# A GLU block's down projection in seven half-size products, beside a spectral filter: one edit to a tuned kernel

## The chip, the cores and the metric

The kernel runs on one core of a Trainium2 chip. The metric is device time in microseconds (us) of one execution. Below, PE is the matmul engine, PEld its weight loads, DVE the vector engine, ACT the scalar engine, POOL the GpSimd engine and SP the sync engine, which here only starts DMAs. "SPq" and "ACTq" are the DMA-starting parts of those engines.

## The reference, cut to what matters

The output is the sum of three things: the input `x` (2048 rows of 512), a spectral filter of its layer norm, and a gated MLP of the same layer norm.

```python
def _A_ref(x, w_r, w_i):
    X = jnp.fft.rfft2(x.astype(jnp.float32), axes=(-2, -1)) * (w_r + 1j * w_i)
    return jnp.fft.irfft2(X, s=(S, D), axes=(-2, -1)).astype(jnp.bfloat16)

def _B_ref(x, w_gate, w_up, w_down):      # 512 -> 1792 -> 512
    h = _gelu(jnp.einsum("bsd,df->bsf", x, w_gate)) * jnp.einsum("bsd,df->bsf", x, w_up)
    return jnp.einsum("bsf,fd->bsd", h, w_down)

xn = _layernorm(A_x)
return A_x + _A_ref(xn, A_w_r, A_w_i) + _B_ref(xn, B_w_gate, B_w_up, B_w_down)
```

## The kernel before, in words

**Rows.** The 2048 rows lie in SBUF as `x_sb`, 16 row blocks `j` of 128 rows by 512 columns (bf16). Four blocks form a chunk `b` (0 to 3). `x_sb` is also the accumulator: the MLP's result and the filter's result `y` are each added into block `j`, and when both are in (`part_done`, twice per block), two DMAs on SP write the block out.

**The MLP.** A loop over chunks and, in each, over 14 slices `fc` of the hidden dimension. `gate` (L685) runs four matmuls of 128x512 into a PSUM bank, ACT applies gelu into `gl` (L688); `up` (L700) runs four more into another bank, and DVE multiplies the two into `hT` (L706), of which there are two, for odd and even chunks. `down(b, jj)` (L738) takes one row block: 14 matmuls with a 128x128 piece of `hT` as weights and 512 columns of `wd` moving, all into one bank, then one DVE add into `x_sb` (`add_to`, L640). The downs of chunk b−1 run inside chunk b, after fc 2, 5, 8 and 11; those of chunk 3 come after everything else. The very last block is split into two column halves (`last_down`, L721), each with its own adds and outputs: first half, then second half.

**The filter.** It is spread through the MLP as small stages: D and A (forward transforms, with a round trip through DRAM: `scr1`, read back as `tv`), B (L570) and the product with the loaded filter `W` (DVE, L581), C (L595, another round trip through DRAM: `scr2`, read back as `vv` into `arena`), E (L619) and F (L649). `W` comes in eight steps `s` of eight 64 KB loads, half on POOL's queue and half on SP's, into a ring of four places (`load_W`); `keep_256` (L559, POOL) saves one column of each. E of block j is copied out by ACT (L626), POOL overwrites one row of it (L628), F reads it, ACT copies F's bank out (L655), and four DVE operations of 256 columns (L665 to L668, a quartet below) make `y`, which a fifth (L640) adds into `x_sb`.

**The order.** Each engine works strictly through its own list, written in program order. What belongs where is set by hand: a counter of "hooks" goes up after every gate, every up, and three times in each down; `at(h, call)` puts a small stage at hook h, and `later`/`flush` put DVE work off until after the next up. B starts at hook 60 and every 4.6 hooks, E at 113 and every 2.2 hooks, F four hooks after E. The helper `op` derives semaphore waits from named keys: a reader waits for the last writer of a key, a writer for its readers too. The block's accumulator has one key, `("acc", j)`. `take` hands out PSUM banks (eight of 512 f32 columns) by a planner's own estimate of when each is free; the real waits come from the keys.

**The end.** After chunk 3's fc there are four downs in a row with a few F stages between; the last adds are followed by output DMAs, on SP and, for half of the last block, on ACT.

Of the kernel before, what the change touches and what calls it, by code (L numbers as in the profile page):

```python
# [13 lines left out]
S = 2048  # L14
# [200 lines left out]
def bass_parallel_sum__spectral_gfnet__glu_gated_geglu__prompt_kernel(  # L215
# [27 lines left out]
    with ExitStack() as es:  # L243
        def sb(name, shape, dt):
            return es.enter_context(nc.sbuf_tensor(name, shape, dt))
# [23 lines left out]
        ev1 = cmx[:, 0:1024].rearrange("p (a c) -> p a c", a=2)  # L269
        xn = cmx[:, 1024:3072].rearrange("p (a d) -> p a d", a=4)  # L270

        W = [[sb("W%d_%d" % (k, i), [P, 2, 2, 258], BF16) for i in range(4)] for k in range(2)]
        w256 = sb("w256", [P, 2, 2, NJ], BF16)
        early = sb("early", [P, 8192], F16)
        xs = [early[:, 512 * i:512 * i + 512] for i in range(8)]
# [10 lines left out]
        zt = [late[:, 512 * i:512 * i + 512].rearrange("p (a t) -> p a t", a=4) for i in range(NZ)]  # L286
        eo = [late[:, 2048 + 512 * i:2560 + 512 * i] for i in range(2)]
        uvt = [late[:, 3072 + 512 * i:3584 + 512 * i] for i in range(2)]
        ys2 = [late[:, 4096 + 512 * i:4608 + 512 * i] for i in range(2)]
        TVK = [("tv", m, r) for m in range(4) for r in range(2)]  # L290
        z256 = late[:, 5120:7168]
        row = sb("row", [32, 64], BF16)
# [6 lines left out]
        mhalf = sb("mhalf", [P, 4], F32)  # L299
        vpe = sb("vpe", [P, NJ], F32)  # L300
        rstd = sb("rstd", [P, NJ], F32)
        dumm = sb("dumm", [P, 512], F16)
        warm_o = sb("warm_o", [P, 1], F32)

# [3 lines left out]
        def bank(i):  # L308
            return psum[:, i * 512:(i + 1) * 512]
# [11 lines left out]
        def take(n, dur, hold=None, ops=1):  # L321
            i = min(range(9 - n), key=lambda i: max(free[i:i + n]))
            pt[0] += dur
            if hold is None:
                act_t[0] = max(act_t[0], pt[0] + 0.25) + 0.2 + 0.43 * n
                end = act_t[0]
            else:
                end = pt[0] + hold
            for k in range(i, i + n):
                free[k] = end  # L330
            return i

        def dma(eng, dst, src, r=(), w=()):
            return op(eng, lambda e: e.dma_start(dst, src), r=r, w=w, dma=True)  # L334
# [293 lines left out]
            op("pool", lambda e: e.tensor_copy(z[0:1, 1, :], z256[0:1, P * j:P * j + P]), r=["z256"], w=[zk])  # L628

        done = {}  # L630

        def part_done(j):

            done[j] = done.get(j, 0) + 1
            if done[j] == 2:
                for b in range(2):
                    dma("sp", ov[b, :, j, :], x_sb[64 * b:64 * b + 64, j, :], r=[("acc", j)], w=[("out", j, b)])

        def add_to(j, src, r, cs=slice(0, D), key=None):
            op("dve", lambda e: e.tensor_tensor(x_sb[:, j, cs], src, x_sb[:, j, cs], ALU.add), r=r + [("acc", j), ("x", j, 0), ("x", j, 1)], w=[("acc", j)])  # L640

        def unit_F(j):
            bk = take(1, 0.23)

            def fn(e):
                z = zt[j % NZ]
                ins = None
                for a in range(4):
                    ins = e.matmul(bank(bk)[:, a * P:(a + 1) * P], z[:, a, :], gm[:, a, :], start=(a == 0), stop=(a == 3), skip_group_check=True)  # L649
                return ins  # L650

            op("pe", fn, r=["gm", ("zt", j % NZ)], w=[("ps", bk)])
            o2 = eo[j % 2]
            ok = ("eo", j % 2)
            op("act", lambda e: e.activation(o2, bank(bk), ACT.Copy), r=[("ps", bk)], w=[ok] + (TVK if j < 2 else []))  # L655
            uv = uvt[j % 2]
            uk = ("uv", j % 2)
            ys = ys2[j % 2]
            yk = ("ys", j % 2)
            u2 = uv.rearrange("p (i h c) -> p i h c", i=2, h=2)  # L660
            neg = ys[:, ::-1].rearrange("p (i h c) -> p i h c", i=2, h=2)[:, :, 0, :]
            pos = ys.rearrange("p (i h c) -> p i h c", i=2, h=2)[:, :, 0, :]

            def fin():
                op("dve", lambda e: e.tensor_tensor(uv[:, 0:256], o2[:, 0:256], o2[:, 256:512], ALU.add), r=[ok], w=[uk + (0,)])  # L665
                op("dve", lambda e: e.tensor_tensor(uv[:, 256:512], o2[:, 0:256], o2[:, 256:512], ALU.subtract), r=[ok], w=[uk + (1,)])
                op("dve", lambda e: e.tensor_tensor(pos, u2[:, :, 0, :], u2[:, :, 1, :], ALU.add), r=[uk + (0,), uk + (1,)], w=[yk + (0,)])
                op("dve", lambda e: e.tensor_tensor(neg, u2[:, :, 0, :], u2[:, :, 1, :], ALU.subtract), r=[uk + (0,), uk + (1,)], w=[yk + (1,)])  # L668

                add_to(j, ys, [yk + (0,), yk + (1,)])  # L670
                part_done(j)
            later.append(fin)

# [36 lines left out]
            else:  # L710
                mult()

        def last_down(bk):
            for c in range(2):
                cs = slice(256 * c, 256 * c + 256)
                bc = (bk + c) % 8

                def fn(e, cs=cs, bc=bc):
                    ins = None
                    for fc in range(NFC):  # L720
                        ins = e.matmul(bank(bc)[:, 0:256], hT[1][:, fc, 3 * P:4 * P], wd_sb[:, fc, cs], start=(fc == 0), stop=(fc == NFC - 1))  # L721
                    return ins
                op("pe", fn, r=[("wd", fc) for fc in range(NFC)] + [("hT", 1, fc, 3) for fc in range(NFC)], w=[("ps", bc)])
                add_to(NJ - 1, bank(bc)[:, 0:256], [("ps", bc)], cs)
                for b, eng in ((0, "sp"), (1, "act")):
                    dma(eng, ov[b, :, NJ - 1, cs], x_sb[64 * b:64 * b + 64, NJ - 1, cs], r=[("acc", NJ - 1)], w=[("out", NJ - 1, b, c)])
            for _ in range(3):
                hook()

        def down(b, jj):  # L730
            j = 4 * b + jj
            bk = take(1, 0.0, 1e9)

            def part(f0, f1):
                def fn(e):
                    ins = None
                    for fc in range(f0, f1):
                        ins = e.matmul(bank(bk), hT[b % 2][:, fc, jj * P:(jj + 1) * P], wd_sb[:, fc, :], start=(fc == 0), stop=(fc == NFC - 1))  # L738
                    return ins
                pt[0] += 0.217 * (f1 - f0)  # L740
                op("pe", fn, r=[("wd", fc) for fc in range(f0, f1)] + [("hT", b % 2, fc, jj) for fc in range(f0, f1)], w=[("ps", bk)])

            if j == NJ - 1:
                return last_down(bk)
            part(0, 5)
            hook()
            part(5, 10)
            hook()
            part(10, 14)
            free[bk] = pt[0] + 1.2  # L750

            add_to(j, bank(bk), [("ps", bk)])
            part_done(j)
            hook()
# [4 lines left out]
        def at(h, *calls):  # L759
            plan.setdefault(int(h), []).extend(calls)  # L760
# [5 lines left out]
        def hook(fl=True):  # L766
            for f, *a in plan.pop(hk[0], []):
                f(*a)
            hk[0] += 1
            if fl:  # L770
                flush()
# [3 lines left out]
            at(10 + 2 * i, (load_late, wd_sb[:, f0:f1, :], wdv[:, f0:f1, :], [("wd", fc) for fc in range(f0, f1)]))  # L775
        at(18, (load_late, be[:], c_be.ap(), ["be"]))
        at(19, (load_late, mm[:], c_mm.ap(), ["mm"]))
        for s, h0 in enumerate((22, 30, 53, 59, 65, 70, 74, 79)):
            for i, t in enumerate(load_W(s)):
                at(h0 + i // 2, t)  # L780
            at(h0 + 9 if s > 1 else 53 + s, (keep_256, s))
        cmv = c_cm.ap().rearrange("p (h r c) -> p h r c", h=NJ, r=2)
        for i, h0 in enumerate((52, 62, 71, 80)):
            hs = slice(4 * i, 4 * i + 4)
            at(h0, (load_late, cm[:, hs], cmv[:, hs], [("cm", 2 * i), ("cm", 2 * i + 1)], (["ev1"], ["ev1", ("xn", 0)], [("xn", 1), ("xn", 2)], [("xn", 2), ("xn", 3)])[i]))
        at(60, (load_late, gm[:], c_g.ap().rearrange("p (a c) -> p a c", a=4), ["gm"]))
# [20 lines left out]
                at(h + 7, (mini, 0))  # L807
            at(h + 8 + (4 if m < 1 else 0), (load_tv, m))
        for g in range(9):
            h = int(60 + 4.6 * g)  # L810
            if g < 8:
                at(h, (unit_B, g))
            if g > 0:
                at(h, (unit_C, g - 1))
                if g > 1:
                    at(h, (load_vv, g - 2))
            if g == 1:
                at(h, (mini, 1))
            if g == 8:
                at(h - 2, (mini, 4))  # L820
                at(h, (mini, 2))
        at(100, (mini, 3))
        at(101, (load_vv, 7))
        for j in range(NJ):
            at(113 + 2.2 * j, (unit_E, j))
            at(117 + 2.2 * j, (unit_F, j))

        def trans1(j):
            for i, eng in enumerate(("dve", "act")):
# [39 lines left out]
        trans(0, (2, 3), (2, 3), "act")  # L869
        gate(0, 5, (0, 1))  # L870
        up(0, 5, (0, 1))
        NH = 6
        for b in range(4):
            for fc in range(NFC):
                jjs = (2, 3) if b == 0 and fc < NH else (0, 1, 2, 3)
                gate(b, fc, jjs)
                hook(False)
                up(b, fc, jjs)
                flush()
                hook()  # L880
                if b > 0 and fc in (2, 5, 8, 11):
                    down(b - 1, (fc - 2) // 3)
        for jj in range(4):
            down(3, jj)
        assert not plan
        pr.wait_all_dma("sp", [ev for k, ev in pr.writer.items() if k[0] == "out"])

# [49 lines left out]
```

## Time and profile before

| | |
|---|---|
| median of 4 runs | 188.79 us (188.01 to 189.7) |
| the profiled execution's own time | 189.7 us |
| its span, first to last instruction | 187.9 us |
| mean granted PE clock | 0.998 |
| PE, DVE, ACT, POOL busy | 96%, 59%, 47%, 21% of the span |
| chunk 3's loop, about | 132 to 171.5 us |
| last output DMA landed | 187.42 us |

The profiled execution's time has 1.8 us around the span that no instruction fills. Lines of the profile name a line of the kernel, an engine and operation, and the tiles as out<-in; "x28" is a count. Matmul records overlap, because their ends are modelled, and a few are missing: L738 has 197 records of 210. So a matmul's price is the distance from one start to the next, not its duration. Where an answer says "[0.84 <-PE ps L721]", the engine was idle for 0.84 us before, until that instruction released it.

### The profile page before, as it was taken

The numbers are of one execution on the slowest core, as the hardware profiler recorded it, in microseconds if no ns is written. First come the engines' busy times: TensorE is split into PE (matmuls) and PEld (weight loads), VectorE is DVE, ScalarE is ACT, GpSimd is POOL, SyncE is SP. The second block draws the span as 40 slices with busy tenths as digits, with TensorE's granted clock in tenths as the row PEclk, the third lists the DMA queues.
The fourth block names the chain that finished last, engine by engine and source line by source line (L and its number), as shares of the span: only waits on it lengthen the run. The fifth ranks groups of instructions, "written<-read, shape, count | busy, mean of one in ns | idle before, by whom it ended". The sixth has DMA issues, their size and how long they took to land.

```text
span 187.9 us, 3460 instructions
## 1 busy us (share of the span) xinstructions
PE 179.6 (96%) x1271; PEld 95.3 (51%) x1284; DVE 110.7 (59%) x262; ACT 88.9 (47%) x143; POOL 39.7 (21%) x90
## 2 busy tenths in 40 slices
PE   7879999999999999999999999999999999999991
PEld 2358755565655444444444444444555555555460
DVE  3476989998362242446645554523259879699520
ACT  1334547766656431455734555513265566654100
POOL 2110081824000007534656200000011111110000
PEclk9999999999999999999999999999999999999999
DMA  4999999798989149756799997420002212211111
GB/s 116 267 247 283 292 272 308 200 184 138 194 112 174 32 100 138 155 143 163 154 223 158 181 221 169 115 57 0 0 3 56 56 45 70 58 37 24 28 42 42
DMA packets 24977, 24.71 MB, mean 132 GB/s; under 512 B 2832, under 2 KB 22800, under 8 KB 24704
## 3 DMA queue, kind: packets, MB, share of 16 engines
q1 hardware_dynamic: 20992, 18.24, 45.3%
q0 software_dynamic: 1968, 5.14, 11.8%
q10 hardware_dynamic: 2000, 1.11, 2.1%
q8 instruction: 10, 0.16, 0.4%
q14 instruction: 7, 0.06, 0.1%
HBM read 18.19 MB, written 6.29 MB: 130 GB/s over the span
## 4 chain that ended last, share of the span: by engine, by line
PE 80%; DVE 8%; DMA 6%; issue 2%; SPq 2%; POOL 1%; ACT 0%; DVEq 0%
PE ps L738 24%; PE ps L700 22%; PE ps L685 21%; DMA wu<-in_B_w_up_dram 5%; DVE st L380 3%; SPq L334 2%; PE ps L595 2%; PE ps L649 2%; PE ps L619 2%; PE ps L570 1%; DVE hT L706 1%; PE ps L402 1%; DMA out_dram<-x_sb 1%; PE ps L471 1%; PE ps L721 1%
## 5 line engine op out<-in xcount | busy, mean ns | idle before, releaser
L700 PE MATMUL ps<-xnT,wu 128*128 128x512 f16 (+1 forms) x248 | 58.6, 359 | 1.1 <-DMA wu<-in_B_w_up_dram 1.0
L685 PE MATMUL ps<-xnT,wg 128*128 128x512 f16 (+1 forms) x248 | 58.6, 359 | 0.7 <-DMA wg<-in_B_w_gate_dram 0.6
L706 DVE TENSOR_TENSOR hT<-ps,gl 128x512 bf16<-128x512 f32 (+1 forms) x62 | 39.4, 636 | 33.7 <-PE ps L700 29.2
L688 ACT ACTIVATE gl<-ps 128x512 bf16<-128x512 f32 (+1 forms) x62 | 34.5, 556 | 46.4 <-PE ps L685 45.6
L738 PE MATMUL ps<-wd,hT 128*128 128x512 bf16 x197 | 46.5, 379 | 0.9 <-issue 0.3
L685 PEld LDWEIGHTS ps<-xnT,wg 128*128 128x128 bf16 x248 | 23.2, 98 | 22.2 <-issue 1.2
L700 PEld LDWEIGHTS ps<-xnT,wu 128*128 128x128 bf16 x248 | 23.3, 98 | 21.7 <-DMA wu<-in_B_w_up_dram 1.9
L738 PEld LDWEIGHTS ps<-wd,hT 128*128 128x128 bf16 x210 | 19.7, 98 | 21.9 <-issue 1.0
L640 DVE TENSOR_TENSOR x_sb<-ps,x_sb 128x512 bf16<-128x512 f32 (+1 forms) x17 | 11.2, 659 | 21.0 <-PE ps L738 17.5
L337 POOL DMA_DIRECT2D W<-in_A_w_r_dram x32 | 18.6, 612 | 13.0 <-PE ps L685 7.8
L628 POOL COPY tv<-tv 1x128 bf16<-1x128 bf16 x16 | 4.5, 284 | 55.2 <-ACT tv L626 55.2
L581 DVE TENSOR_TENSOR early<-early,W 128x1024 bf16<-128x1024 f16 x16 | 10.3, 687 | 7.2 <-ACT early L576 7.2
L655 ACT ACTIVATE tv<-ps 128x512 bf16<-128x512 f32 x16 | 9.5, 595 | 9.8 <-PE ps L649 9.8
L380 DVE BATCH_NORM_STATS2 st<-x_sb 128x6 f32<-128x512 bf16 x16 | 10.5, 681 | 3.9 <-DMA x_sb<-in_A_x_dram 3.9
L447 ACT ACTIVATE early<-ps 128x512 f16<-128x512 f32 x16 | 9.5, 595 | 5.4 <-PE ps L443 5.4
L576 ACT ACTIVATE early<-ps 128x1024 f16<-128x1024 f32 x8 | 8.2, 1023 | 6.5 <-PE ps L570 6.5
L626 ACT ACTIVATE tv<-ps 128x512 bf16<-128x512 f32 x16 | 9.6, 598 | 3.0 <-PE ps L619 3.0
L479 ACT ACTIVATE early<-ps 128x1024 f16<-128x1024 f32 x8 | 7.9, 1022 | 4.6 <-PE ps L474 3.8
L388 POOL TENSOR_TENSOR rstd<-vpe,mhalf 128x4 f32<-128x4 f32 (+1 forms) x5 | 4.5, 901 | 23.7 <-DVE vpe L387 23.7
L600 ACT ACTIVATE early<-ps 128x1024 bf16<-128x1024 f32 x8 | 8.2, 1020 | 0.8 <-PE ps L595 0.8
L392 DVE TENSOR_SCALAR cmx<-x_sb,ag,rstd 128x512 f16<-128x512 bf16 x16 | 6.1, 420 | 2.1 <-POOL rstd L388 2.1
L640 DVE TENSOR_TENSOR x_sb<-tv,x_sb 128x512 bf16<-128x512 bf16 x16 | 6.8, 424 | 0.6
(75 smaller groups left out, 145.4 us busy)
## 6 DMA issues: line engine op xcount, KB each, us to landing
W<-in_A_w_r_dram POOLq DMA_DIRECT2D x32, 64.2 KB, 3.6
W<-in_A_w_i_dram SPq DMA_DIRECT2D x32, 64.2 KB, 5.1
tv<-scr SPq DMA_DIRECT2D x8, 256.0 KB, 5.2
scr<-early SPq DMA_DIRECT2D x8, 256.0 KB, 4.2
arena<-scr SPq DMA_DIRECT2D x8, 256.0 KB, 5.7
out_dram<-x_sb SPq DMA_DIRECT2D x30, 64.0 KB, 2.0
scr<-early SPq DMA_DIRECT2D x14, 128.0 KB, 3.6
x_sb<-in_A_x_dram SPq DMA_DIRECT2D x6, 256.0 KB, 11.8
```

Of the source, the lines that this page charges most:

```text
L337: op(eng, lambda e: e.dma_start(dst, src), w=list(keys) + list(also), dma=True, after=[("pe", pr.cnt["pe"])])
L380: op("dve", lambda e: e.bn_stats(st[:, j, :], x_sb[:, j, :]), r=[("x", j, 0), ("x", j, 1)], w=[("st", j)])
L447: op("act", lambda e: e.activation(x4.rearrange("p (a c r) -> p a c r", a=2, r=4), bank(bk).rearrange("p (a r c) -> p a c r", a=2, r=4), A ...
L581: op("dve", lambda e, k=k: e.tensor_tensor(pp[i][k], xc[i], W[k][g % 4][:, :, :, 0:256], ALU.mult), r=[("xc", i)] + [key for c in range(2) ...
L626: op("act", lambda e: e.activation(z, bank(bk).rearrange("p (a c) -> p a c", a=4), ACT.Copy, scale=SC_E), r=[("ps", bk)], w=[zk] + (TVK if ...
L640: op("dve", lambda e: e.tensor_tensor(x_sb[:, j, cs], src, x_sb[:, j, cs], ALU.add), r=r + [("acc", j), ("x", j, 0), ("x", j, 1)], w=[("ac ...
L655: op("act", lambda e: e.activation(o2, bank(bk), ACT.Copy), r=[("ps", bk)], w=[ok] + (TVK if j < 2 else []))
L685: ins = e.matmul(bank(bg)[:, 0:n], wg_sb[:, dc, fc * P:(fc + 1) * P], xnT[:, dc, c0:c0 + n], start=(dc == 0), stop=(dc == 3))
L688: op("act", lambda e: e.activation(gl[k % 3][:, 0:n], bank(bg)[:, 0:n], ACT.Gelu_apprx_tanh), r=[("ps", bg)], w=[("gl", k % 3)])
L700: ins = e.matmul(bank(bu)[:, 0:n], wu_sb[:, dc, fc * P:(fc + 1) * P], xnT[:, dc, c0:c0 + n], start=(dc == 0), stop=(dc == 3))
L706: op("dve", lambda e: e.tensor_tensor(hT[b % 2][:, fc, h0:h0 + n], bank(bu)[:, 0:n], gl[k % 3][:, 0:n], ALU.mult), r=[("ps", bu), ("gl", k ...
L738: ins = e.matmul(bank(bk), hT[b % 2][:, fc, jj * P:(jj + 1) * P], wd_sb[:, fc, :], start=(fc == 0), stop=(fc == NFC - 1))
```

## The change

The down projection of chunks 2 and 3 is done in another way; chunks 0 and 1 keep `down`. A chunk's rows are cut in two halves of two blocks, the hidden dimension in two halves of seven fc, and the 512 output columns in two halves. A 2x2 block product needs eight half products; the identity used here needs seven, with sums of the operands: four sums of `wd` (`T`, once), four sums of `hT` (`S`, once per chunk), and sums of the results. This is done for p = 0 and 1, the two blocks of a half.

- `product(b, p, step)`: seven matmuls of 256 columns per step, seven steps. Two PSUM banks `bx` and `by` are held over all seven. After step 0 ACT copies bx to by; after step 3 it copies by to bx. Steps 1 and 4 end in a DVE add of a column half into `x_sb`; steps 2 and 3 in a DVE add of bank and `x_sb` into a new f32 tile `tw` ("base"); steps 5 and 6 in a DVE add of bank and `tw` into `x_sb`.
- Chunk 2's 14 steps stand one after each fc of chunk 3 (p = 0, then p = 1). Chunk 3's 14 steps stand at the end, p = 0 and 1 in turn within each step. `last_down` goes.
- `sums_T` at hooks 92 to 98, `sums_S` of chunk 2 at 100 to 108, of chunk 3 after fc 7 to 13. The `W` ring becomes one tile, whose place `T` takes over; `S` takes over the place of `early`, `xnT` and `cmx`. In chunks 2 and 3 the fc are taken in the order 0, 7, 1, 8, and so on, so that both halves of a sum come early.
- `y` is no longer added by DVE: POOL starts a DMA of 128 KB from `ys` to `x_sb` that accumulates, two hooks after the quartet. `ys` has four buffers instead of two. Between a block's base and the end of its products its `y` add is held back ("locked").
- The accumulator's key is split by column half. Chunk 3's outputs are written per half: 14 DMAs of half width on SP and 2 on ACT.
- Hooks: W loads of s = 2, 3 come at 34 and 40 instead of 53 and 59, the others 2 to 4 hooks earlier, B starts at 58, E at 105 and every 2.6 hooks, F 3.5 hooks after E.

```diff
-        W = [[sb("W%d_%d" % (k, i), [P, 2, 2, 258], BF16) for i in range(4)] for k in range(2)]
+        wring = sb("wring", [P, 8 * 1032], BF16)
+        W = [[wring[:, 1032 * (4 * k + i):1032 * (4 * k + i) + 1032].rearrange("p (r h c) -> p r h c", r=2, h=2) for i in range(4)] for k in range(2)]
+        T = [wring[:].bitcast(F16)[:, 1792 * k:1792 * k + 1792].rearrange("p (f c) -> p f c", f=7) for k in range(4)]
...
+        def sums_S(b, f0, f1, ks):
...
+            for k in ks:
+                a, b2, o, r = ((A(1, 0), A(1, 7), ALU.add, hk(0, 1) + hk(7, 1)),
+                               (ssum(b, 0, f0, f1), A(0, 0), ALU.subtract, s_keys(b, 0, f0, f1) + hk(0, 0)),
+                               (A(0, 0), A(1, 0), ALU.subtract, hk(0, 0) + hk(0, 1)),
+                               (A(0, 7), ssum(b, 1, f0, f1), ALU.subtract, hk(7, 0) + s_keys(b, 1, f0, f1)))[k]
...
+        def product(b, p, step):
...
+            bx, by = wb[p]
+            bk = (bx, bx, by, by, bx, by, by)[step]
...
+                for f in range(7):
+                    ins = e.matmul(o, st_(f), mv(f), start=(f == 0 and step in (0, 5)), stop=(f == 6), skip_group_check=True)
...
+            def out_half(j, hh):
+                if last:
+                    for bb, eng in ((0, "sp"), (1, "act" if step == 6 else "sp")):
+                        dma(eng, ov[bb, :, j, 256 * hh:256 * hh + 256], x_sb[64 * bb:64 * bb + 64, j, 256 * hh:256 * hh + 256], r=[("acc", j, hh)],
...
+            def copy(dst, src):
+                return op("act", lambda e: e.activation(bank(dst)[:, 0:256], bank(src)[:, 0:256], ACT.Copy), r=[("ps", src)], w=[("ps", dst)], after=war(("ps", dst)))
+
+            def base(t, j, *after):
+                locked[j] = []
+                op("dve", lambda e: e.tensor_tensor(t, o, x_sb[:, j, 256:512], ALU.add), r=rk + [("acc", j, 1), ("x", j, 0), ("x", j, 1)], w=[("tw", p, j == jA)],
...
+            if step == 0:
+                copy(by, bx)
+            elif step == 1:
+                add_to(jA, o, rk, 0)
+                out_half(jA, 0)
+            elif step == 2:
+                base(t12, jA)
+            elif step == 3:
+                base(t22, jB, copy(bx, by))
+            elif step == 4:
+                add_to(jB, o, rk, 0)
+                out_half(jB, 0)
+            elif step == 5:
+                add_to(jB, o, rk + [("tw", p, False)], 1, t22)
+                out_half(jB, 1)
+                release(jB)
+            else:
+                add_to(jA, o, rk + [("tw", p, True)], 1, t12)
+                out_half(jA, 1)
+                release(jA)
...
-                add_to(j, ys, [yk + (0,), yk + (1,)])
+                at(hk[0] + 2, (add_y,))
+
+            def add_y():
+                if j in locked:
+                    locked[j].append(add_y)
+                    return
+                op("pool", lambda e: e.dma_start(x_sb[:, j, :], ys, accum_op=ALU.add), r=[yk + (0,), yk + (1,), ("x", j, 0), ("x", j, 1)] + acc(j),
+                   w=acc(j), dma=True)
                 part_done(j)
...
-        for s, h0 in enumerate((22, 30, 53, 59, 65, 70, 74, 79)):
+        for s, h0 in enumerate((20, 27, 34, 40, 61, 66, 70, 75)):
...
-            h = int(60 + 4.6 * g)
+            h = int(58 + 4.6 * g)
...
-            at(113 + 2.2 * j, (unit_E, j))
-            at(117 + 2.2 * j, (unit_F, j))
+            at(105 + 2.6 * j, (unit_E, j))
+            at(108.5 + 2.6 * j, (unit_F, j))
...
+            for n, fc in enumerate(range(NFC) if b < 2 else [7 * (i % 2) + i // 2 for i in range(NFC)]):
...
-                if b > 0 and fc in (2, 5, 8, 11):
-                    down(b - 1, (fc - 2) // 3)
-        for jj in range(4):
-            down(3, jj)
+                if b in (1, 2) and n in (2, 5, 8, 11):
+                    down(b - 1, (n - 2) // 3)
+                if b == 3:
+                    product(2, n // 7, n % 7)
+                    for call in S3.get(n, ()):
+                        sums_S(3, *call)
+        for step in range(7):
+            for p in range(2):
+                product(3, p, step)
```

## The prediction

> **What bounds the kernel now.** I read the page first (busy shares, slices, chain of waits), then the windows of the last third, then the order of time at the end, then the groups by form for prices.
>
> ```profile
> PE 179.6 (96%) x1271; PEld 95.3 (51%) x1284; DVE 110.7 (59%) x262; ACT 88.9 (47%) x143; POOL 39.7 (21%) x90
> ...
> DVE  3476989998362242446645554523259879699520
> ...
> PE 80%; DVE 8%; DMA 6%; issue 2%; SPq 2%; POOL 1%; ACT 0%; DVEq 0%
> ```
>
> A busy PE alone proves little, but the chain agrees: four fifths of it is PE, the rest mostly the start. The DVE slices show where the second limit is near: 9s in the last quarter, over chunk 3.
>
> ```profile
> 146.00:158.00 12.00, 11.95 (x86) 6.62 (x85) 9.85 (x30) 7.12 (x14) 1.47 (x5) 1.00 0.23 56
> 158.00:172.00 14.00, 13.89 (x100) 7.75 (x100) 11.97 (x36) 9.32 (x17) 1.68 (x6) 1.00 0.20 48
> ```
>
> Columns: stretch, length, then busy PE, PEld, DVE, ACT, POOL, clock, DMA share. PE has no holes at full clock; DVE is 82% and 86% busy. So PE work taken out here is time won, as long as DVE keeps up.
>
> ```profile
> 174.51 6.21 PE L738 MATMUL ps<-wd,hT 128*128 128x512 bf16 x28
> ...
> 180.55 3.22 PE L721 MATMUL ps<-wd,hT 128*128 128x256 bf16 x28
> ...
> 182.28 0.42 DVE L640 TENSOR_TENSOR x_sb<-ps,x_sb 128x256 bf16<-128x256 f32 x1 [0.84 <-PE ps L721]
> 182.74 3.16 ACTq L334 DMA_DIRECT2D out_dram<-x_sb  x2
> 184.94 0.42 DVE L640 TENSOR_TENSOR x_sb<-ps,x_sb 128x256 bf16<-128x256 f32 x1 [2.23 <-DMA out_dram<-x_sb]
> ```
>
> Order of time (start, length). Matmuls overlap, so the slot is (length − one)/(n − 1): (6.21 − 0.379)/27 = 0.216 us for 512 columns, (3.22 − 0.272)/27 = 0.109 us for 256. PE's last slot ends at 183.61. The last DVE add comes only at 184.94: it waits for the first half's output DMA, since both halves share one key. The last output lands at 187.42, 3.81 after PE; the span closes 0.48 later.
>
> **The change, part by part.**
>
> *Products (won).* A chunk's down projection takes 56 slots of 0.216 = 12.08 us; in chunk 3, 42 of them and 28 of 0.109 = 12.12. After: 7 products × 7 matmuls × 2 row pairs = 98 slots of 0.109 = 10.70. Two chunks: 24.20 − 21.40 = **2.80 us** off PE. Weight loads double per column; in the 28 half-size slots each load (98 ns) hid under 109 ns, so nothing is added. A rule speaks against this. The Trainium skill, "TensorE: Matmul & The Clock Gate", section "Back-to-back issue gap", puts a sustained stream of load and matmul at about 81 ns for 128 columns and 131 ns for 512: on a straight line, an estimate of 98 ns for 256, so 98 × 98 ns = 9.6 against 56 × 131 ns = 7.3, and each chunk would *lose* 2.3 us. This trace has 0.216 and 0.109 for the same tiles; the rows decide.
>
> *DVE (moved and added).*
>
> ```profile
> L706 DVE TENSOR_TENSOR hT<-ps,gl 128x512 bf16<-128x512 f32 x50 | 34.3, 688 | 31.1 <-PE ps L700 27.3 <-ACT gl L688 2.2 <-PE ps L685 1.1
> L581 DVE TENSOR_TENSOR early<-early,W 128x1024 bf16<-128x1024 f16 x16 | 10.3, 687 | 7.2 <-ACT early L576 7.2
> L640 DVE TENSOR_TENSOR x_sb<-tv,x_sb 128x512 bf16<-128x512 bf16 x16 | 6.8, 424 | 0.6
> L665 DVE TENSOR_TENSOR tv<-tv 128x256 bf16<-128x256 bf16 x16 | 4.6, 286 | 0.7 <-ACT tv L655 0.5
> L640 DVE TENSOR_TENSOR x_sb<-ps,x_sb 128x256 bf16<-128x256 f32 x2 | 0.8, 425 | 3.1 <-DMA out_dram<-x_sb 2.2 <-PE ps L721 0.8
> ```
>
> (Busy us, mean ns, idle before.) Operand sums are 16-bit tensor_tensor like L581 and L665: 0.687 for 1024 columns, 0.42 for 512, 0.285 for 256; on that line 1792 columns are 1.1. T: 4 × 1.1 = 4.4. S: 4 × (0.687 + 0.42 + 0.285) = 5.6 per chunk. Product adds: 12 × 0.425 = 5.1 per chunk for 2.7 before. The y adds go: −6.8. Net +13.6 us of DVE. T and chunk 2's S fall into 122 to 134 us, where DVE is busy 4.25 of 12: hidden. Chunk 3 is where cover is thin. Per fc PE needs 8 × 0.216 + 7 × 0.109 + about 0.44 for E and F, some 3.0 us; for the six fc where S(3) runs I count 18.0. DVE in those: six hT (4.1), seven y quartets (8.1), five adds (2.1), S (4.4): 18.8 by mean durations, 16.7 by starts, since in the order of time hT is followed after 0.60 and a quartet takes 1.05. So DVE is 93 to 104% full: a lag of 0 to 0.8 us. Behind a late DVE stand first the hT banks, six now where seven were; with 4.3 groups an fc a bank comes round after 6/4.3 × 3.0 = 4.2 us, of which its up, the hand-over and hT use 1.8, so PE feels a lag above about 2.3. Next is the tail (chunk 3's products, nothing else on PE). Counted from its start DVE ends the last hT at 0.13, the quartet at 1.2, the last add at 1.6, S at 2.7, two adds at 3.7, and then waits for step 2 until 4.0: some 0.4 to spare before step 3. I take **+0.2**.
>
> *y by DMA.* 16 accumulating transfers of 128 KB on POOL; none is in the trace.
>
> ```profile
> gm<-c_g POOLq DMA_DIRECT2D x1, 128.0 KB, 2.9
> ```
>
> That is the nearest row: same queue, size and partitions, 2.9 us to landing. Bounds: 2.3 (the quickest 64 KB W load on POOL) and 5.8 (twice, as the destination is read too); I take 3.5, nearer to the row. A gain below that is excluded by none but does nothing. Behind the waiting POOL instruction stand only the z copies (L628) of later E, due three hooks later, about 3 us: covered. Who waits for a landing: row 9 (y issued after step 1's add, row base at step 2, one fc later: 3.1 us, of which 0.7 goes before the issue) leaves 2.5 for the transfer, so DVE stands 1.0 at 3.5; and row 15 in the tail, which leaves about 5.5. The first adds to DVE's lag and is worked off in part over the four fc left: **+0.3** for PE. The Trainium skill, "SBUF — State Buffer", section "Who interferes with whom", says that a VectorE op with two SBUF inputs shuts out a GpSimd op that reads SBUF for its whole length, so each issue could slip by one op, up to 0.69. The 16 z copies took 279 to 349 ns beside such quartets: no such slip here, at most 0.07. By the rule row 9 would cost 0.4 more; I leave it in the range.
>
> *ScalarE copies between banks.* 8 of 128x256, like the 383 ns gelu of that size: 3.1 us. In chunk 3 each has an fc to finish. In the tail PE does the other row pair meanwhile: 7 × 0.109 = 0.764. A hand-over costs 0.20 from the last slot to the reader's start (182.08 to 182.28), 0.38 or 0.425 for the copy or add, 0.06 back: 0.64 to 0.69. It fits by 0.08. **+0.1**; if it missed by 0.1 everywhere, four steps × two pairs, +0.8.
>
> *The end.* Halves get their own keys, so the wait of 184.94 goes (183.61 + 0.2 instead). But SP now issues 14 half-size outputs, two per row half.
>
> ```profile
> L334 SPq DMA_DIRECT2D out_dram<-x_sb x32: 466/526/816, 141.2 to 185.4; - x32
> ```
>
> A pair takes about 0.51 + 0.60 = 1.1 on SP (min/median/max above). From step 4 four pairs fall due every 0.764 us but take 1.1, so SP is 1.1 behind when step 6's last one is due, 0.66 after PE: it starts 1.75 after PE's end and lands 1.8 later, 3.55 against 3.81. **−0.25**. With issues of 0.3 it would be −1.1, with 0.66 each +0.8.
>
> *Moved W loads, earlier B and E.* B's first unit comes one gate and up (1.73) earlier: 76.0 instead of 77.74. It waits for the last tv load, which landed at 75.94 (issued 69.84, 6.1). That is on time with nothing left over; the W loads of s=2,3 that now run at about 49 to 62 instead of 72 to 84 could delay the spectrum's stores before it, but DMA stood nearly idle at 62 to 64, and the four tv pairs took 4.3 to 4.6 and 5.9 to 6.2 at any load: +0.1, bound +1.5. E's first unit waits for the last vv load: 9.84 us after C(7) starts, and by the new order E starts 10.9 after it: covered by 1.1. The SP order (row, then vv) is unchanged there.
>
> *Sum.* −2.80 + 0.2 + 0.3 + 0.1 − 0.25 + 0.1 = **−2.35**. The profiled execution's span is 187.9, with 1.8 around it (189.7): it would be 185.55 and 187.35. That run is 0.9 above the median of the four, so I take the difference from the median: 188.79 − 2.35 = **186.4 us**.
>
> **Rivals.**
>
> *R1, the accumulate lands late (slower).* Place: row 9's base in DVE's queue, and row 15's in the tail. With D us to landing the loss is D − 2.5 less some 1.7 that banks and later fc absorb for row 9, and D − 5.5 for row 15, against a gain of 2.85 without either wait and DVE's lag: 2D − 9.7 = 2.85, so it decides from D = 6.3. For: POOL's loads took 6.5 to 8 us while the DMA engines were full (90 to 107 us), and an accumulate is unknown. Against: here DMA is 0.2 busy and 2.9 is the row. At 7.5 the loss is 5.3, so 188.8 − 2.85 + 5.3 = 191.2.
>
> *R2, the gain turns into waits, no change.* DVE over 100% in chunk 3 (sums on every fc, in-order waits for the product's end) and SP's backlog at 0.66 an issue: +0.8 lag into the tail, +0.8 hand-overs, +0.3 at B instead of my small terms, SP +0.8: −2.80 + 0.8 + 0.8 + 0.3 + 0.8 = −0.1, about 188.4 at the worst, 188.0 as its middle. For: 93 to 104%. Against: chunk 3 before ran at 86% without a hole in PE.
>
> *R3, the end is fully won.* Issues on SP overlap, no stall: −2.80 − 1.1 = −3.9: 184.9.
>
> *That the half-size products save nothing* (the rule above) is a fourth: +4.5, 193; the 28 slots of 0.109 leave it 2 in 100, counted with R1.
>
> **How the numbers follow.** Main case 0.50, own range 185.4 to 187.4; R3 0.12; R2 0.20; R1 with the fourth 0.18. A measurement of this kernel (188.0 to 189.7 over four runs) can hardly tell less than 1%, so the bounds are 186.9 and 190.7. Faster: R3 and three quarters of the main case, 0.49. Slower: nearly all of R1, 0.16. Same: the rest, 0.35. The range 184.8 to 190.0 leaves out R1's larger part (0.15) and a little below.
>
> **What would show it.** Right: 98 slots of 0.109 in the last 10.7 us of PE, gate and up unchanged, no DVE wait on a DMA over 1 us, last landing about 3.5 after PE. Wrong: product slots above 0.12; DVE base (x_sb into tw) waiting for the y DMA by several us; holes before the steps of the tail above 0.1; PE waiting before the first B (tv) or E (vv). The prediction falls if landings of the y DMA pass 6 us, or if DVE's lag reaches the hT banks.

## The result, and the profile after

The changed kernel takes 188.28 us (median of 35 runs, 187.3 to 194.06), the kernel before 188.91 (56 runs, 187.95 to 189.91): a ratio of 0.9969, with a 95% interval of 0.9955 to 0.9983. That is 0.6 us less (0.3 to 0.85), where 2.35 less was predicted. The sign is right, the size is a quarter of the forecast. Two of the 35 runs were slow ones with a lower PE clock (190.59 us at 0.988 and 194.06 at 0.977, the others 0.992 or more); here and below such runs count in the medians and not in the ratios.

The profiled execution took 189.13 us, with a span of 187.24 (187.9 before). First the page: busy shares, DVE by slices, and the chain of waits by engine.

```profile
PE 176.5 (94%) x1346; PEld 102.3 (55%) x1354; DVE 121.0 (65%) x289; ACT 91.8 (49%) x151; POOL 53.3 (28%) x106
...
DVE  3566999997452242355635556998687678797750
...
PE 73%; DMA 11%; DVE 7%; SPq 2%; issue 2%; ACT 1%; POOL 1%; ACTq 0%; DVEq 0%
```

PE lost 3.1 us of busy time, but its share of the chain fell from 80% to 73%, while DMA rose from 6% to 11%. So some of the time that PE no longer works is now spent waiting for transfers. DVE's busy time grew by 10.3 us. The sum of its operations' durations grew by 13.2, where 13.6 was predicted; neighbouring operations overlap in the record. Its slices over chunk 3 have 6 to 9, as before.

Where DMA came in is seen in the order of time (start, length) around the first B unit, L573:

```profile
74.32 1.03 PE L836 MATMUL ps<-xnT,wu 128*128 128x512 f16 x4
...
77.23 0.41 PE L573 MATMUL ps<-tv,be 64*64 64x256 f16 x8 [1.89 <-DMA tv<-scr]
```

The four matmuls of `up` fill their slots until 74.32 + 4 × 0.216 = 75.19. B starts at 77.23, 2.05 later, released by the last `tv` load, which landed at 76.89. PE shows about 0.09 at every switch to these 64x64 tiles, so the wait is 1.95 us. Before, this place had no wait.

The second place is the end, in the order of time, and then SP's own queue from the same stretch:

```profile
171.29 3.22 PE L720 MATMUL ps<-wd,hT 128*128 128x256 bf16 x28
172.99 0.29 DVE L797 TENSOR_TENSOR tv<-tv 128x256 bf16<-128x256 bf16 x1 [1.17 <-DMA x_sb<-tv]
174.40 3.23 PE L720 MATMUL ps<-wring,xnT 128*128 128x256 f16 x28
...
180.52 1.69 PE L720 MATMUL ps<-wd,cmx 128*128 128x256 bf16 x14
181.94 1.26 ACTq L337 DMA_DIRECT2D out_dram<-x_sb  x2
182.25 0.42 DVE L649 TENSOR_TENSOR x_sb<-ps,tw 128x256 bf16<-128x256 f32 x1 [0.34 <-PE ps L720]
```

```profile
178.88 6.51 SPq L337 DMA_DIRECT2D out_dram<-x_sb  x10
```

The products do what they should: a slot is (3.22 − 0.272)/27 = 0.109 us, and 28 slots from 171.29 end at 174.35, where the next 28 begin at 174.40. PE's last slot ends at 180.52 + 14 × 0.109 = 182.05 and the last add at 182.67. But SP is still starting output DMAs: ten of them, the first at 178.88, the last at 184.80, so 5.92/9 = 0.66 us from one to the next. The last one lands at 186.70, 4.65 after PE's end, where it was 3.81 before.

The two profiled spans in one sum (us):

| | before | after | difference |
|---|---|---|---|
| span start to the first D matmul | 20.80 | 20.11 | −0.69 |
| from there to PE's last slot, without the wait before B | 162.81 | 159.99 | −2.82 |
| wait before the first B | 0 | 1.95 | +1.95 |
| PE's last slot to the last landing | 3.81 | 4.65 | +0.84 |
| last landing to the end of the span | 0.48 | 0.54 | +0.06 |
| span | 187.9 | 187.24 | −0.66 |

The first row is not the change's: the instructions there are the same, and it varied from 19.57 to 20.80 over the profiles of this study. The wait before B varies too: with these hooks it was 1.95, 0.67, 1.31, 0.54, 1.26 and 1.03 in six profiles (the change and five experiments below), a mean of 1.1. With that mean and without the first row the sum is −2.8 + 1.1 + 0.9 = −0.8, against −0.6 by medians.

### The profile page after: what moved, and what is told of

It reads as the page before. It is cut to its first block, busy times and chain, and to the rows that moved or that the text cites. A ratio compares the mean times of both kernels' runs of the same rounds, so it can differ in the third digit from the quotient of the medians.

```text
span 187.2 us, 3669 instructions
## 1 busy us (share of the span) xinstructions
PE 176.5 (94%) x1346; PEld 102.3 (55%) x1354; DVE 121.0 (65%) x289; ACT 91.8 (49%) x151; POOL 53.3 (28%) x106
## 4 chain that ended last, share of the span: by engine, by line
PE 73%; DMA 11%; DVE 7%; SPq 2%; issue 2%; ACT 1%; POOL 1%; ACTq 0%; DVEq 0%
PE ps L836 19%; PE ps L821 19%; PE ps L720 11%; PE ps L857 11%; DMA wu<-in_B_w_up_dram 4%; DMA tv<-scr 3%; DMA scr<-early 3%; DVE st L383 3%; SPq L337 2%; PE ps L598 2%; PE ps L622 2%; PE ps L779 2%; PE ps L573 1%; DVE hT L842 1%; PE ps L405 1%
## 5 line engine op out<-in xcount | busy, mean ns | idle before, releaser
L857 PE MATMUL ps<-wd,hT 128*128 128x512 bf16 x104 | 24.4, 379 | 0.4
L340 POOL DMA_DIRECT2D wring<-in_A_w_r_dram x32 | 18.5, 611 | 13.3 <-PE ps L857 5.6
L857 PEld LDWEIGHTS ps<-wd,hT 128*128 128x128 bf16 x112 | 10.8, 98 | 12.4 <-issue 0.2
L649 DVE TENSOR_TENSOR x_sb<-ps,x_sb 128x512 bf16<-128x512 f32 (+1 forms) x16 | 8.8, 553 | 9.6 <-PE ps L857 9.3
L805 POOL DMA_DIRECT2D x_sb<-tv x16 | 13.5, 863 | 3.9 <-DVE tv L798 2.5
L584 DVE TENSOR_TENSOR early<-early,wring 128x1024 bf16<-128x1024 f16 x16 | 10.3, 687 | 5.9 <-ACT early L579 5.9
L383 DVE BATCH_NORM_STATS2 st<-x_sb 128x6 f32<-128x512 bf16 x16 | 10.6, 680 | 3.3 <-DMA x_sb<-in_A_x_dram 3.3
L562 POOL COPY w<-wring 128x4 bf16<-128x4 bf16 x16 | 3.9, 251 | 20.1 <-DMA wring<-in_A_w_r_dram 11.4
```

The lines of the kernel that those rows point to most:

```text
L340: op(eng, lambda e: e.dma_start(dst, src), w=list(keys) + list(also), dma=True, after=[("pe", pr.cnt["pe"])])
L383: op("dve", lambda e: e.bn_stats(st[:, j, :], x_sb[:, j, :]), r=[("x", j, 0), ("x", j, 1)], w=[("st", j)])
L584: op("dve", lambda e, k=k: e.tensor_tensor(pp[i][k], xc[i], W[k][g % 4][:, :, :, 0:256], ALU.mult), r=[("xc", i)] + [key for c in range(2) ...
L805: op("pool", lambda e: e.dma_start(x_sb[:, j, :], ys, accum_op=ALU.add), r=[yk + (0,), yk + (1,), ("x", j, 0), ("x", j, 1)] + acc(j), w=ac ...
```

## The experiments

The theory behind the first experiments had three parts: products −2.8; B, set at hook 58, waits for `tv`, and the W loads moved to hooks 34 and 40 are what delays `tv`; SP's rate of issue ends the kernel late. The rivals: B at 58 is too early at any load; the end is bound by something other than SP (the adds, the write itself); DVE is so full that the gain is lost there unless the `y` adds stay off it. All ratios are to the kernel before, on the same chip.

**The W loads late again (`e1_w_late`).** All loads of `W` back at the old hooks, B still at 58.

```diff
-        for s, h0 in enumerate((20, 27, 34, 40, 61, 66, 70, 75)):
+        for s, h0 in enumerate((22, 30, 53, 59, 65, 70, 74, 79)):
...
-            at(h0 + 9 if s > 3 else 47 + s, (keep_256, s))
+            at(h0 + 9 if s > 1 else 53 + s, (keep_256, s))
```

> The changed kernel with the W loads and keep_256 at the hooks of the kernel before (W of s=2,3 at 53 and 59 again); B still starts at hook 58. Theory (the early W loads share the DMA engines with the chunk 2 read-back and the last spectrum stores, so the last tv load is late): the 2.05 us that PE stood before the first B falls to 0.3 or less, the stores of group 3 take 2.5 to 3.8 us again instead of 4.8 to 5.3, time about 186.4, ratio to before 0.987. Rival (B at hook 58 is too early for the tv load whatever else runs): PE still stands 1 us or more there, time 187.8 to 188.3.

Measured: 187.89 us, ratio 0.9950 (0.9917 to 0.9982). In its order of time:

```profile
76.43 0.41 PE L573 MATMUL ps<-tv,be 64*64 64x256 f16 x8 [1.11 <-DMA tv<-scr]
```

B still waits: it starts 1.27 us after the slots before it end, 1.18 without the switch of 0.09. The stores ahead of `tv` did get quicker (2.4 to 4.1 us to landing, where the change had 4.8 to 5.3), but `tv` landed at 76.08, after B's turn. So the early loads are not the cause, or not alone: B at 58 is too early without them. Whether they add to it stays open. From the issue of the last stores to the landing of `tv` it takes 10.3, 10.3 and 11.1 us in the three profiles with late loads (the kernel before, `e8_before_split` and this one), and 10.5 to 11.9, mean 11.1, in the ten with early loads: half a microsecond more, but the ranges overlap.

**The last outputs shared with ACT (`e3_out_act`).** The second DMA of each pair goes to ACT's queue in every step.

```diff
-                    for bb, eng in ((0, "sp"), (1, "act" if step == 6 else "sp")):
+                    for bb, eng in ((0, "sp"), (1, "act")):
```

> The changed kernel with one of the two outputs of every row half of chunk 3 issued by ACT instead of SP. Theory (14 half-size outputs at 0.64 us each on SP are what ends the kernel): the last landing comes 2.8 to 3.2 us after PE's last slot instead of 4.65, time about 186.7, ratio 0.988. Rival (the writes themselves, or the engines behind the queues, are the limit): last landing still 4.3 us or more after PE, time 188.0 to 188.4. A third way: ACT's copies between banks stand behind its own DMA issues (0.5 us each) and PE gets holes in the tail, time 187.5 or more with holes of 0.3 us.

Measured: 186.32 us, ratio 0.9865 (0.9835 to 0.9895); run again as `e12_out_act_b`, 186.18 and 0.9852. The order of time at its end, SP and ACT side by side:

```profile
177.55 4.29 SPq L337 DMA_DIRECT2D out_dram<-x_sb  x6
177.56 4.44 ACTq L337 DMA_DIRECT2D out_dram<-x_sb  x6
...
179.19 1.69 PE L720 MATMUL ps<-wd,cmx 128*128 128x256 bf16 x14
...
180.92 0.42 DVE L649 TENSOR_TENSOR x_sb<-ps,tw 128x256 bf16<-128x256 f32 x1 [0.34 <-PE ps L720]
```

PE ends at 179.19 + 14 × 0.109 = 180.72, and the last output lands at 183.42: 2.70 after PE instead of 4.65. Tiles, adds and bytes are the same; only the queue differs. Nor did ACT's own copies suffer from its DMA starts: PE has no gap above 0.06 us between the steps of the tail. SP's rate was the end's bound, worth 1.95 us; by medians (0.9865 and 0.9852 against 0.9969) 2.0 and 2.2.

**`y` added by DVE as before (`e4_y_dve`).** The accumulating DMA becomes the old DVE add.

```diff
-                op("pool", lambda e: e.dma_start(x_sb[:, j, :], ys, accum_op=ALU.add), r=[yk + (0,), yk + (1,), ("x", j, 0), ("x", j, 1)] + acc(j),
-                   w=acc(j), dma=True)
+                add_to(j, ys, [yk + (0,), yk + (1,)])
```

> The changed kernel with y added into x_sb by DVE again (same hooks, same holding back) instead of the accumulating DMA. DVE gets 16 adds of 0.42 us back, 6.8 us. Theory (DVE was near full in chunk 3 and the DMA add is what made room; the DMA itself costs PE nothing): DVE's lag reaches the hT banks or the tail, PE gets 1 to 4 us of holes after 140 us, time 189 to 192. Rival (the DMA add costs by its own waits, DVE has room): no holes, time 187.5 to 188.3.

Measured: 188.12 us, ratio 0.9938 (0.9917 to 0.9958). The windows late in chunk 3 (stretch, length, busy PE, PEld, DVE, ACT, POOL, clock, DMA share, GB/s), first of the change, then of this run:

```profile
156.00:170.00 14.00, 14.00 (x113) 9.22 (x112) 12.45 (x37) 8.66 (x16) 4.97 (x10) 1.00 0.35 63
```

```profile
156.00:170.00 14.00, 14.00 (x110) 8.97 (x108) 13.65 (x41) 8.78 (x16) 1.43 (x4) 1.00 0.08 20
```

DVE is busy 13.65 of 14 us, 97%, and PE still has no hole; nor has it one above 0.25 us anywhere after 78 us. From the first D matmul to PE's last slot, without the wait before B, it takes 159.99 us, the same as in the change. So the theory's holes did not come, DVE could have kept the adds, and moving them to a DMA won nothing on the path. Whether it cost a little is open: the two intervals (up to 0.9958, from 0.9955) just meet.

**The moved hooks alone (`e5_before_moved`).** The kernel before, with only the new hooks of W, of its companion copies and loads, and of B with C and the small stages that follow it.

```diff
-        for s, h0 in enumerate((22, 30, 53, 59, 65, 70, 74, 79)):
+        for s, h0 in enumerate((20, 27, 34, 40, 61, 66, 70, 75)):
...
-            h = int(60 + 4.6 * g)
+            h = int(58 + 4.6 * g)
```

> The kernel before with only the new hooks of the W loads, of keep_256, of the cm loads and of B (58), C and the small stages beside them; downs, adds, E and F as they were. Theory (the new hooks alone make the wait): PE stands 1.3 to 2.3 us before the first B, time about 190.6, ratio 1.009. Rival (the wait comes from the products' or y's part of the change): no wait over 0.3 us, time 188.9.

Measured: 189.62 us, ratio 1.0038 (1.0017 to 1.0059), so +0.7 us; its profile has a wait of 0.54 before B. The hooks alone make the kernel slower, with no product changed. The wait is less than the theory's 1.3 to 2.3 us and more than the rival's 0.3: the profile of the change, with its 1.95, was at the high end of what this wait takes.

**B two hooks later (`e6_b60`), and both repairs (`e7_b60_act`).** B starts at 60 again, and what follows it is moved along; in the second the outputs are shared with ACT as well.

```diff
-            h = int(58 + 4.6 * g)
+            h = int(60 + 4.6 * g)
...
-            at(105 + 2.6 * j, (unit_E, j))
-            at(108.5 + 2.6 * j, (unit_F, j))
+            at(107 + 2.5 * j, (unit_E, j))
+            at(110.5 + 2.5 * j, (unit_F, j))
```

> The changed kernel with B at hook 60 as before, C, the small stages and the last vv load 2 hooks later with it, T and S of chunk 2 one or two hooks later, E at 107 and every 2.5 hooks, F at 110.5 and every 2.5. The early W loads stay. Theory (the chain from the last spectrum stores to the last tv load takes 10.3 to 11.9 us, B at 58 leaves it 10.2): with 1.73 us more PE stands at most 0.2 us before the first B in a typical execution, time about 187.2 to 187.5, 0.8 to 1.1 less than the changed kernel. Rival (the wait is only moved: PE stands as long before E, C or the products instead): time 188.0 to 188.5.

> B at hook 60 as in e6_b60 and the second output of every row half of chunk 3 issued by ACT as in e3_out_act. If both costs are separate they add: 188.3 - 1.0 - 1.95 = 185.3, ratio 0.981. If they overlap, 186.0 or more.

Measured: 187.48 us, ratio 0.9919 (0.9886 to 0.9951), and 186.15 us, ratio 0.9847 (0.9801 to 0.9892). The first is what was expected. The second is not the 185.3 of two costs that add, and which of the two readings holds is taken up again below. First `e6_b60` around B, then `e7_b60_act` in the tail:

```profile
75.95 1.03 PE L836 MATMUL ps<-xnT,wu 128*128 128x512 f16 x4
...
76.91 0.41 PE L573 MATMUL ps<-tv,be 64*64 64x256 f16 x8
```

```profile
171.38 0.29 DVE L797 TENSOR_TENSOR tv<-tv 128x256 bf16<-128x256 bf16 x1 [1.35 <-DMA x_sb<-tv]
```

The wait before B is gone: 75.95 + 0.86 = 76.81, and B at 76.91. But a smaller one came: E and F are later now, so row 15's quartet waits 1.35 us for its buffer. That buffer is one of the four `ys`, and the held-back `y` transfer of row 11 still reads it. Behind the quartet in DVE's queue stands the last S sum, and step 2 of the tail waits 0.36 for it. In the change itself the same DVE wait is 1.17 (shown above) and PE's other row pair hides all but 0.05 of it.

**One hook instead of two, and both again (`e10_b59_act`, `e11_b60_act_b`, `e12_out_act_b`).** B at 59 with outputs shared; and repeats of `e7_b60_act` and `e3_out_act` on one chip.

```diff
-            h = int(58 + 4.6 * g)
+            h = int(59 + 4.6 * g)
```

> The changed kernel with ACT issuing the second outputs and B, C, the small stages and the last vv load one hook later (B at 59, a gate of 0.86 us later); T, S, E and F as in the change. If PE's wait before the first B is a matter of the chain from the last stores (10.3 to 11.9 us, now against 11.1), it falls to 0 to 0.8 us and nothing else moves (the vv load has 0.2 us to spare before E): time about 185.6, between e3_out_act (186.3) and 185.2. If the wait returns before E instead, 186.3 again.

> The kernel of e7_b60_act once more, for a narrower interval: its profile accounts for 187.3 - 2.83 (products) + 0.36 (a hole before step 2 in the tail) - 1.11 (end) = 183.7 us of span, 185.5 us of time, where four runs gave 186.15. If the two costs add, 185.3 to 185.8; if the second gain is lost elsewhere, 186.1 or more.

> The kernel of e3_out_act once more, on the same chip as the two others: 186.3. The difference to e11_b60_act_b is what the wait before B costs in the median, less 0.36: 0.4 to 0.9 if it is 0.8 to 1.3 in a typical execution.

Measured: 186.03 us, ratio 0.9831 (0.9798 to 0.9865); 186.05 us, 0.9833 (0.9802 to 0.9864); 186.18 us, 0.9852 (0.9826 to 0.9877). `e10_b59_act` around B and, later, the first E:

```profile
75.93 0.41 PE L573 MATMUL ps<-tv,be 64*64 64x256 f16 x8
...
125.93 0.38 PE L622 MATMUL ps<-be,arena 128*128 128x128 f16 x4 [0.39 <-DMA arena<-scr]
```

In this one profile B no longer waits (the chain before it took 10.9 us, and B at 59 leaves 11.1), but C's round trip is later with E left where it was, and a hole of 0.55 opens before E. In the traces the third (B at 58) has 161.02 us from the first D matmul to PE's last slot, the first two 160.54 and 160.38. The medians differ by 0.15, with intervals several times as wide, and the expected times (185.6, and 185.3 to 185.8) and difference (0.4 to 0.9) were missed: that the two repairs add up is seen in the traces, and not settled in the times. The best of these are near 186.05, 1.5% below the kernel before.

**The end of the kernel before, repaired (`e8_before_split`).** The kernel before, in which only the two halves of the last block get keys of their own.

```diff
-                add_to(NJ - 1, bank(bc)[:, 0:256], [("ps", bc)], cs)
+                op("dve", lambda e, cs=cs, bc=bc: e.tensor_tensor(x_sb[:, NJ - 1, cs], bank(bc)[:, 0:256], x_sb[:, NJ - 1, cs], ALU.add), r=[("ps", bc), ("acc", NJ - 1)], w=[("acc2", c)])
...
-                    dma(eng, ov[b, :, NJ - 1, cs], x_sb[64 * b:64 * b + 64, NJ - 1, cs], r=[("acc", NJ - 1)], w=[("out", NJ - 1, b, c)])
+                    dma(eng, ov[b, :, NJ - 1, cs], x_sb[64 * b:64 * b + 64, NJ - 1, cs], r=[("acc2", c)], w=[("out", NJ - 1, b, c)])
```

> The kernel before with only the last block's two halves under keys of their own, so that the last DVE add does not wait for the first half's output. Theory: last landing 2.7 us after PE's last slot instead of 3.81, time 1.1 less than before, ratio 0.994. Rival (the second half's outputs then queue behind the first half's, so nothing is won): landing 3.5 us or more after PE, ratio 0.999.

Measured: 187.87 us, ratio 0.9929 (0.9900 to 0.9958).

```profile
180.25 3.22 PE L721 MATMUL ps<-wd,hT 128*128 128x256 bf16 x28
...
183.51 0.42 DVE L724 TENSOR_TENSOR x_sb<-ps,x_sb 128x256 bf16<-128x256 f32 x1 [1.10 <-PE ps L721]
```

The last add no longer waits for a DMA; the last output lands 2.71 after PE's end instead of 3.81. So the key's split, one of the small parts of the change, is worth 1.1 us by the trace and 1.3 by the ratio, alone. The change took it in and gave it back in SP's queue. The new down projection by itself is then to be held against this kernel: 186.05 against 187.87, or 1.8 us, with the two intervals together 1.0 to 2.6.

**Whole-row outputs (`e9_out_whole`).** An output only when a block's second half is in: six DMAs of whole rows on SP, two on ACT.

```diff
-                if last:
+                if last and hh:
...
-                        dma(eng, ov[bb, :, j, 256 * hh:256 * hh + 256], x_sb[64 * bb:64 * bb + 64, j, 256 * hh:256 * hh + 256], r=[("acc", j, hh)],
-                            w=[("out", j, bb, hh)])
+                        dma(eng, ov[bb, :, j, :], x_sb[64 * bb:64 * bb + 64, j, :], r=acc(j), w=[("out", j, bb)])
```

> The changed kernel with chunk 3's outputs written as whole row blocks: 6 DMAs on SP and 2 on ACT instead of 14 and 2; the first half of a block waits for the second. If the number of DMAs on SP in the last 5 us is what ends the kernel, the last landing comes 2.8 to 3.1 us after PE and the time is about 186.6, as with ACT's help. If it is the bytes or their late start, landing stays above 4 us after PE and the time at 188 or more.

Measured: 187.97 us, ratio 0.9938 (0.9915 to 0.9962); the last landing is 3.56 after PE. Both expectations missed; it came between. The order of time shows why:

```profile
179.48 3.75 SPq L337 DMA_DIRECT2D out_dram<-x_sb  x6
...
181.01 1.29 ACTq L337 DMA_DIRECT2D out_dram<-x_sb  x2
181.32 0.42 DVE L649 TENSOR_TENSOR x_sb<-ps,tw 128x256 bf16<-128x256 f32 x1 [0.34 <-PE ps L720]
```

Half as many DMAs still come due together, in steps 5 and 6, and six issues, from 179.48 to 182.55, are 0.61 us apart. The last add ends at 181.74, but SP comes to its output only at 182.55: that delay is most of the 0.86 that this end takes longer than `e3_out_act`'s 2.70. Twice the bytes cost less: 2.13 us from the last issue to its landing, 1.90 in the change. So the number of issues on one queue within the last 2 to 3 us counts for more than their bytes.

By the ratios this is worth 0.6 us, with the two intervals together 0.1 to 1.1, so no more than the 1.1 of the landing. Spans alone should not be compared here: this profiled execution has 2.5 us of time outside its span, that of the change 1.9. A stretch of 2.4 us or more outside the span occurs in 15 of 110 executions with the new down projection and in none of 109 with the old one; what makes it is not shown.

## Why the prediction was wrong, by its own steps

The step that failed first is **"Moved W loads, earlier B and E", +0.1**. It took the landing of `tv` at 75.94 as a fixed time and set B's new turn of 76.0 beside it: "on time with nothing left over". That landing is the end of a chain: the last stores are issued, they land, `tv` is issued, it lands. From the issue of the stores to the landing it took 10.3 us before, and 11.9, 11.1, 10.6 and 10.5 in the change, `e1_w_late`, `e3_out_act` and `e5_before_moved`; the new hooks leave B 10.2. Another 0.35 passes from the landing to B's first matmul (76.89 to 77.23 in the change), which the prediction left out: with the chain of 10.3 as it was, B would already have waited about 0.3. With the new hooks B waited 0.5 to 2.0 us, mean 1.1. `e5_before_moved` has the hooks alone (+0.7), `e6_b60` removes the wait. The text allowed +1.5 as a bound and took +0.1: a margin of nothing was priced near nothing.

The second is **"The end", −0.25**, which came out at +0.84, and +0.9 with the span's close. The mechanism was right (keys split, then SP late) and the price per issue was wrong: 0.55, near the old median of 0.526, where SP works back to back and takes 0.66. Over nine steps that is 1.0 us, and the last output starts 2.75 after PE's end, not 1.75. "With 0.66 each +0.8" stood in the text as the worse bound. The row it used was of outputs spread over 44 us; the case to be priced was a queue that never empties. `e3_out_act` shows the cause and its size (−1.95), `e8_before_split` what the end could have been (2.71).

What held:

- *Products, −2.80*: −2.82 by PE's slots. The slots are 0.109 us, each with its own weight load. The figures that the prediction took from the Trainium skill, "TensorE: Matmul & The Clock Gate", section "Back-to-back issue gap", by which each chunk would lose 2.3 us, do not hold for this stream, and the fourth rival falls with them.
- *DVE, +0.2*: nothing on PE's path. The sums cost what their rows said (first row below: 1.08 for 1792 columns); PE has no hole above 0.25 us in chunk 3, even in `e4_y_dve` at 97%.
- *y by DMA, +0.3*: landing after 2.6 to 4.3 us, median 2.7, with 2.3 to 5.8 given. No base waited, so R1's case, which begins at 6.3, did not come. What did come was not in the text: row 15's quartet waits for its *buffer*, 1.17 us, under cover here and 0.36 out of cover in `e6_b60`.
- *ScalarE copies, +0.1*: 0.369 each (second row below), and PE's only gap between the steps of the tail is the 0.05 named above.

Groups of the change, by form (count, busy us and mean ns, idle before and what ended it):

```profile
L691 DVE TENSOR_TENSOR wring<-wd 128x1792 f16<-128x1792 bf16 x2 | 2.2, 1082 | 0.0
...
L742 ACT ACTIVATE ps<-ps 128x256 f32<-128x256 f32 x8 | 3.0, 369 | 7.7 <-PE ps L720 7.7
```

One reading was half wrong, at no cost to the time. "No such slip here" looked at the lengths of POOL's copies alone. In the kernel before, three operations L667 that began just after such a copy took 0.36 to 0.42 us instead of 0.29, so there it was DVE that waited (first two lines). In the change a copy that begins inside an `S` sum takes 0.57 instead of 0.28 (last two):

```profile
168.26 0.28 POOL L628 COPY tv<-tv 1x128 bf16<-1x128 bf16 x1 [2.11 <-ACT tv L626]
168.28 0.42 DVE L667 TENSOR_TENSOR tv<-tv 128x256 bf16<-128x256 bf16 x1
```

```profile
164.65 0.68 DVE L685 TENSOR_TENSOR cmx<-hT,xnT 128x1024 f16<-128x1024 bf16 x1
164.91 0.57 POOL L631 COPY tv<-tv 1x128 bf16<-1x128 bf16 x1 [2.59 <-ACT tv L629]
```

DVE's operations beside the starts of `y`'s DMA, which the prediction feared for, kept their lengths.

By its sum the prediction said −2.80 + 0.2 + 0.3 + 0.1 − 0.25 + 0.1; measured are −2.82 + 0 + 0 + 0 + 0.9 + about 1.1 = −0.8, and −0.6 by medians. The time is near that of R2, "the gain turns into waits" (188.0), by two of R2's four terms: SP, near its 0.8, and B, at 1.1 instead of 0.3. The other two, DVE's lag and the hand-overs, did not occur, so R2 has the size in part by luck. (R2's sum of −0.1 is 188.7 us at the worst, not the 188.4 in the text.) The remaining 0.2 between the sum and the medians lies within the interval.

## What to carry to other kernels

When a stage is set earlier, do not hold its new turn against the time at which its input landed: add up the chain that makes the input from its first issue, with the spread of each transfer and the hand-over at its end, and price a margin of zero at the spread. Where a change splits its last outputs, count how many DMAs one queue must start in the last microseconds, at its back-to-back rate; a second queue can be worth more than the arithmetic saved. And look first for the cheap part of a large edit: one split key in the old kernel was worth twice what the whole change brought.

## What the runs showed of the hardware

- SP started output DMAs 0.51 us after the first, then 0.64 apart when back to back, and 0.73 to 0.84 while ACT was starting its two; 0.66 on average over nine. Halving their number and doubling their size left 0.61.
- DVE ran at 97% over 14 us without a hole on PE: nearly full is not yet late, so long as no one waits in order behind it.
- An accumulating 128 KB transfer from SBUF to SBUF landed in 2.6 to 4.3 us (median 2.7), at 0.86 us of POOL's time to start it. A plain load of that size on the same queue took 2.9 before and 2.4 in the change, so no cost of reading the destination showed.
- A wait for a round trip through DRAM varied from 0.5 to 2.0 us over six profiles with the same hooks of its loads and its reader.
- A DVE operation with two inputs in SBUF and a POOL copy in SBUF held each other up, whichever began second: 0.42 us instead of 0.29 on DVE, 0.57 instead of 0.28 on POOL.
